# A wider opening, feature-map folds as small products, and finer side steps in a fused attention and SwiGLU kernel

## The chip, the cores and the metric

The kernel runs on one core of a Trainium2 chip. The metric is the device time of one execution in microseconds (us); lower is better. TensorE (PE in the profile) multiplies, VectorE (DVE) and ScalarE (ACT) do element work and read the matmul results in PSUM, GpSimd (POOL) does element work between SBUF tensors only, and SyncE (SP) issues almost all DMAs. Each engine works through its own queue in order.

## The reference, cut to what matters

Two branches read the same normalised tokens `xn` (2048 tokens, 1024 wide): a linear attention with a learned softmax feature map over 32 heads of width 32, and a gated SwiGLU block with 3584 hidden features. The result is `x + attention * silu(swiglu)`, all in float32.

```python
xn = layernorm(x)                                   # 2048 x 1024
q, k, v = split(xn @ wqkv)                          # 32 heads of 32
pq = einsum("bhsd,hdf->bhsf", q, w_phi)             # per head 32 x 32; pk alike
phi = concat([softmax(p), softmax(-p)])
o = phi_q (phi_k^T v) / (phi_q sum(phi_k));  s = o @ wo
h = silu(xn @ w1) * (xn @ w3)                       # 1024 -> 3584
g = silu(h @ w2)                                    # 3584 -> 1024
out = x + s * g
```

Since `q @ w_phi` is `xn @ (wq @ w_phi)` for each head, the kernel multiplies ("folds") `w_phi` into `wq` and `wk` once, before it uses them.

## The kernel before

**Products.** A float32 operand is held as a high part, rounded to the fast format, and a low part, the rest (`split`, L93 to L96: a ScalarE cast makes the high part, a VectorE subtraction the low part). A product takes three passes (high by high, high by low, low by high). The gate and up projections are done by Winograd's form of Strassen's scheme: 512 of 1024 input columns, 512 tokens, and `w1` beside `w3` give a two by two block product, which seven half-size products cover. Their left sides are sums of four token blocks: A11 and A12 (the first 512 tokens, both halves of the columns), A21 and A22 (the next 512), S1 = A21 + A22, S2 = S1 - A11, S3 = A11 - A21, S4 = A12 - S2. Their right sides come from one block of 128 features: B11 and B21 are the halves of `w1`, and T2, T1, T3, B22 and T4 need `w3` as well (`b_sums`, L128, makes two of the sums). One such product is a *step* of `gate_up` (L628): 12 matmuls of 128x512 at L655.

**Order.** For each half of the tokens (`tb`) there are 28 feature blocks `f` with seven products `j` each, 196 steps. The list `events` gives the order of (tb, f, j); j counts A11, A12, S2, S1, S3, S4, A22. Block 0 and 1 are interleaved (`FIRST_PAIR`), later ones follow one by one. All five queues are written out in program order. The right sides of a step are made four steps ahead (`LEAD`, `prep_at`, `sums_at`), their raw weights are loaded two blocks ahead into two buffers (`rw`, L259).

**Opening.** The first 14 steps come while the tokens are still being loaded, normalised (`stats`, `rstd`, `norm`), turned by TensorE (`turn`, L220, four 128x128 transposes into one PSUM bank, `tr`), copied out (ScalarE) and split. Twenty transposes of no use go ahead of all (L749). Steps 0 to 3 need A11 and A12 only. Between them TensorE does 12 of the 32 folds (`first_folds`, L332): four matmuls each against a block-diagonal `bd` (L252), a ScalarE copy and a store. S2 is made and split ahead of S1 (L803 to L811).

**Side work.** From step 14 on, VectorE, ScalarE and SP do work for later stages between the steps: the operands of the second token half (`side_x`), the other folds (`side_fold`: 16 or 32 small matmuls of 32x32 tiles at L532, turned back by VectorE at L538; two units for the rest of `wk`, eight for `wq`), the operands of the key and value products (`side_kv`), stores (`side_store`). `room` (L438) places each item in the first step whose planned VectorE time stays under 2.55 us. `at` puts an item behind the matmuls of a step. `side_fold` holds all three `tr` banks and bank a from its matmuls (L532) to its transposes.

Behind the two token halves come the key and value heads, the query heads, the second SwiGLU product and the output; these stages are the same in both kernels.

## Time and profile before

| | |
|---|---|
| median of 3 runs (lowest to highest) | 2372.14 us (2369.02 to 2375.39) |
| profiled execution, its own time | 2372.7 us |
| its span in the profile | 2370.9 us |
| mean granted TensorE clock | 0.997 |
| TensorE busy | 2345.3 us, 99% |
| VectorE busy | 1774.7 us, 75% |
| ScalarE busy | 897.9 us, 38% |
| GpSimd busy | 257.6 us, 11% |
| DMA | 578.03 MB, 244 GB/s in the mean |

The span is what the profile covers of the execution; 1.8 us lie around it. The busy time of TensorE includes stretches in which matmuls overlap, and its ends are modelled. A row of a timeline gives the start in us, the time it took, the engine, the line of the kernel, the operation, the tiles (written <- read), the shapes and how many instructions were merged, with idle time before it and what ended it in brackets.

### The profile page before, as it was taken

The page shows a single profiled execution, that of the slowest core. Times are in us where ns is not written, and L with a number is a line of the kernel's source. Part 1 is how long each engine was busy: PE and PEld are TensorE (multiplying, and loading weights), DVE is VectorE, ACT ScalarE, POOL GpSimd, SP SyncE. Part 2 cuts the span into 40 slices and gives each one's busy share as a digit, 9 for nine tenths or more (in the row PEclk, how much of TensorE's full clock was granted, in tenths as well). Part 3 has the DMA queues.
Part 4 walks back from the last instruction along what each step waited for, and adds up shares of the span by engine and source line. Part 5 has one row for each costly group of instructions (what it writes and reads, how often), then busy time and mean ns, then how long its engine had stood idle before and what let it go on. Part 6 is the DMA issues. An engine that isn't in the chain of part 4 may idle for free.

```text
span 2370.9 us, 37641 instructions
## 1 busy us (share of the span) xinstructions
PE 2345.3 (99%) x14592; PEld 1922.2 (81%) x14592; DVE 1774.7 (75%) x2777; ACT 897.9 (38%) x1577; POOL 257.6 (11%) x243
## 2 busy tenths in 40 slices
PE   7999999999999999999999999999999999999999
PEld 6788888888888888888788888887888888888787
DVE  8877778886788888874566666777678888787775
ACT  6545444443455455542221222334443333352000
POOL 1000000000000000000000000331012222113562
PEclk9999999999999999999999999999999999999999
DMA  5446689998988888865987878986444653478763
GB/s 215 149 162 218 227 278 310 320 313 281 281 297 297 293 271 301 272 226 191 377 287 287 293 251 316 369 299 249 160 133 143 204 178 133 164 239 281 205 180 103
DMA packets 298354, 578.03 MB, mean 244 GB/s; under 512 B 24624, under 2 KB 151744, under 8 KB 295488
## 3 DMA queue, kind: packets, MB, share of 16 engines
q1 hardware_dynamic: 291840, 552.56, 69.2%
q10 hardware_dynamic: 6336, 23.07, 2.4%
q8 instruction: 115, 1.88, 0.3%
q14 instruction: 63, 0.52, 0.1%
HBM read 372.64 MB, written 202.91 MB: 243 GB/s over the span
## 4 chain that ended last, share of the span: by engine, by line
PE 93%; DVE 3%; DMA 2%; ACT 1%; issue 0%; POOL 0%; SPq 0%; DVEq 0%; ACTq 0%; POOLq 0%
PE bankb L655 24%; PE bankb L1279 13%; PE bankc L655 12%; PE pm L1431 8%; PE bankb L874 7%; PE bankc L1279 6%; PE banka L655 6%; PE bankc L874 3%; PE banka L1279 3%; PE bankb L941 3%; PE banka L874 2%; PE bankc L941 1%; PE po L1416 1%; PE pkv L859 1%; DMA xoA<-xo_d0A 1%; PE banka L941 1%
## 5 line engine op out<-in xcount | busy, mean ns | idle before, releaser
L96 DVE TENSOR_TENSOR bo<-rw,bo 128x512 fp32r<-128x512 f32 x336 | 231.6, 691 | 151.6 <-ACT bo L95 151.3
L1279 PE MATMUL bankb<-bo,as 128*128 128x512 f32 x960 | 235.2, 389 | 1.3 <-ACT acc L1285 1.3
L1279 PEld LDWEIGHTS bankb<-bo,as 128*128 128x128 f32 x960 | 180.1, 188 | 39.1 <-ACT acc L1285 1.7
L95 ACT CAST bo<-rw 128x512 fp32r<-128x512 f32 x336 | 206.7, 618 | 13.4 <-DMA w_d6B<-w2o 3.3
L655 PE MATMUL bankc<-op0S,bo 128*128 128x512 f32 x672 | 163.2, 392 | 0.3 <-DVE op0S L96 0.3
L655 PE MATMUL bankb<-op0S,bo 128*128 128x512 f32 x672 | 162.1, 390 | 1.3 <-ACT op0S L95 0.6
L655 PE MATMUL bankb<-op1S,bo 128*128 128x512 f32 x672 | 161.4, 389 | 0.9 <-ACT u L690 0.9
L655 PE MATMUL bankc<-op1S,bo 128*128 128x512 f32 x672 | 161.5, 389 | 0.1
L655 PE MATMUL bankb<-op0A,bo 128*128 128x512 f32 x672 | 160.6, 394 | 0.7 <-ACT op0A L738 0.7
L1431 PE MATMUL pm<-wos,oT 128*128 128x512 f32 x672 | 160.0, 393 | 0.0
L851 POOL MEMSET ev<- 128x32 f32 x32 | 4.2, 132 | 1419.2 <-DVE bo L96 1083.8
L1279 PE MATMUL bankc<-bo,as 128*128 128x512 f32 x624 | 158.4, 389 | 0.0
L655 PE MATMUL bankb<-op1A,bo 128*128 128x512 f32 x672 | 157.7, 390 | 0.0
L655 PEld LDWEIGHTS bankb<-op0A,bo 128*128 128x128 f32 x672 | 126.5, 190 | 28.2 <-ACT op0A L738 1.1
L655 PEld LDWEIGHTS bankc<-op0S,bo 128*128 128x128 f32 x672 | 125.0, 188 | 29.9 <-issue 2.5
L655 PEld LDWEIGHTS bankb<-op0S,bo 128*128 128x128 f32 x672 | 125.6, 188 | 28.0 <-DVE op0S L96 1.1
L655 PEld LDWEIGHTS bankb<-op1S,bo 128*128 128x128 f32 x672 | 126.0, 188 | 27.5 <-ACT u L690 1.3
L655 PEld LDWEIGHTS bankb<-op1A,bo 128*128 128x128 f32 x672 | 125.8, 188 | 27.5 <-DVE u L698 1.3
L655 PEld LDWEIGHTS bankc<-op1S,bo 128*128 128x128 f32 x672 | 126.0, 188 | 26.6 <-DVE bo L96 0.5
L1431 PEld LDWEIGHTS pm<-wos,oT 128*128 128x128 f32 x672 | 124.8, 188 | 27.4 <-DVE oT L1422 0.3
L1279 PEld LDWEIGHTS bankc<-bo,as 128*128 128x128 f32 x624 | 117.1, 188 | 24.4
L1293 DVE TENSOR_TENSOR acc<-bankb,acc 128x512 f32<-128x512 f32 x152 | 102.0, 685 | 31.2 <-PE bankb L1279 31.2
(272 smaller groups left out, 4333.9 us busy)
## 6 DMA issues: line engine op xcount, KB each, us to landing
rw<-in_w SPq DMA_DIRECT2D x112, 512.0 KB, 4.5
hr<-h_d SPq DMA_DIRECT2D x56, 512.0 KB, 5.4
h_d<-h SPq DMA_DIRECT2D x111, 256.0 KB, 4.9
xoS<-xo_d0S SPq DMA_DIRECT2D x44, 512.0 KB, 6.5
xoS<-xo_d1S SPq DMA_DIRECT2D x44, 512.0 KB, 5.7
xoA<-xo_d0A SPq DMA_DIRECT2D x33, 512.0 KB, 5.2
xoA<-xo_d1A SPq DMA_DIRECT2D x33, 512.0 KB, 4.4
e_d<-eq ACTq DMA_DIRECT2D x32, 512.0 KB, 6.1
```

Of the source, the lines that this page charges most:

```text
L95: nc.scalar.copy(hi, src)
L96: (by or nc.vector).tensor_sub(lo, src, hi.bitcast(F))
L655: nc.tensor.matmul(bank[b], bos[tb, f][bn][:, w, k], ao[an][:, u, k], start=first and n == 0, stop=LAST[b] == an and n == 11, skip_group_c ...
L851: nc.gpsimd.memset(v[:, :, DH:], 1.0)
L859: nc.tensor.matmul(pkv[sl, m], e[:, m // 4, (m % 4) * P + 32 * h:(m % 4) * P + 32 * h + 32], v[:, 4 * (m % 4) + h], start=first and m == 0 ...
L874: nc.tensor.matmul(bank[b], xo[an][:, u, k], wb[bn][:, w, k], start=an in ("A11", "A12", "S1") and n == 0, stop=LAST[b] == an and n == 11, ...
L941: nc.tensor.matmul(bank[b], xo[an][:, u, k], wb[bn][:, w, k], start=an in ("A11", "A12", "S1") and n == 0, stop=LAST[b] == an and n == 11, ...
L1279: nc.tensor.matmul(bank[b], t[:, u, pos + k], bos[kb, bn, k][:, w], start=first and n == 0, stop=LAST[b] == an and n == 5, skip_group_chec ...
L1293: nc.vector.tensor_add(c, pb, c)
L1416: nc.tensor.matmul(po[32 * j:32 * j + 32, a, 64 * k:64 * k + 64], kvs[sl, j, c, k], et[sl, :, 4 * k + j], start=True, stop=True, skip_grou ...
L1431: nc.tensor.matmul(p, oTs[t, h][:, a, k], wos[c, 4 * h + k][:, b], start=n == 0, stop=n == 3 * ND - 1)
```

## The change

The opening covers four feature blocks in place of two, so that steps 0 to 8 (except step 7) need only the token blocks A11 and A12 and the `w1` halves of blocks 0 to 3; blocks 2 and 3 get their right sides B11 and B21 from raw weights put into an unused part of an operand buffer, and a `tr` bank each for their bank b (`kept_banks`). S1 is made and split ahead of S2. Seven low parts of the opening (`first_b` with `nc.gpsimd`) and `b_sums` of blocks 0 and 1 are on GpSimd; in the kernel before only those `b_sums` were. Sixteen more transposes go ahead. The 12 folds against `bd` are gone from the opening; all folds are 16 units of `side_fold` of 16 matmuls each, every one with its own load, transposes and store through one buffer `wf`. The side items of two VectorE instructions become items of one, and the starts of the side work (`FIRST_STEP`, `KV_STEP`, `UNITS`) are new. The three `tr` banks have a name each (`tr_bank`). `wkT` comes from the host in the layout of `wqT`.

```diff
+    def b_sums(b11, b12, b22, t2, eng=None, parts=range(2)):
 
         eng = eng or nc.vector
-        eng.tensor_sub(b12, b22, b12)
-        eng.tensor_add(t2, b12, b11)
+        if 0 in parts:
+            eng.tensor_sub(b12, b22, b12)
+        if 1 in parts:
+            eng.tensor_add(t2, b12, b11)
...
+    turned, kept_banks = [0], {}
+
+    def tr_bank():
+
+        while True:
+            turned[0] += 1
+            if turned[0] % 3 not in kept_banks.values():
+                return dict(tag=f"tr{turned[0] % 3}", bufs=1)
+
+    def turn(half, **kw):
+        pt = ps.tile([P, 4, P], F, name="pt", **(kw or tr_bank()))
...
-    def load_w(wT, dch, c, t=None):
-        wr = blk("wr") if t is None else t
-        nc.sync.dma_start(wr, wT[dch][:, 4 * c:4 * c + 4])
-        return wr
-
-    def fold(wr, c):
-
-        pw = ps.tile([P, 4, P], F, name="pw", tag="tr", bufs=3)
-        for g in range(4):
-            nc.tensor.matmul(pw[:, g, :], wr[:, g], bd[:, 4 * c + g, :], start=True, stop=True)
-        return pw
-
-    folds = [(wkT, k, c, wk_d[c][k]) for c in range(2) for k in range(ND)][:FOLDS]
...
+    def b_operand(bo, n, src, by=None):
+        bo[n] = quad("bo")
+        split(bo[n][:, 0], bo[n][:, 1], src.rearrange("p (k n) -> p k n", n=P), by)
...
+    def b_others(rw, bo, t2=None):
+
+        b11, b21, b12, b22 = rw
+        late = t2 is None
+        if late:
+            t2 = work.tile([P, 512], F, name="t2", tag="w")
+            b_sums(b11, b12, b22, t2)
             yield
         else:
-            hold.append(lambda: b_sums(b11, b12, b22, t2, eng))
-        for _, _, n in ORDER:
-            src = {"B11": b11, "B21": b21, "T2": t2, "T1": b11, "T3": b12, "B22": b22, "T4": b21}[n]
-            bo[n] = quad("bo")
-            split(bo[n][:, 0], bo[n][:, 1], src.rearrange("p (k n) -> p k n", n=P))
-            if n == ("B11" if hold is None else "T2"):
+            nc.vector.tensor_sub(b11, b22, t2)
+        for n in ("T2", "T1", "T3", "B22", "T4") if late else ("T1", "T2", "T3", "B22", "T4"):
+            b_operand(bo, n, {"T2": t2, "T1": b11, "T3": b12, "B22": b22, "T4": b21}[n])
+            if n == "T2" and late:
                 nc.vector.tensor_sub(b11, b22, t2)
-            elif n == ("B21" if hold is None else "B22"):
+            elif n == ("T1" if late else "T3"):
                 nc.vector.tensor_sub(b21, b21, t2)
             yield
...
-    FIRST_PAIR = ((0, 0), (1, 0), (0, 1), (1, 1)) + tuple((f, j) for j in range(2, 7) for f in range(2))
-    events = [(0, f, j) for f, j in FIRST_PAIR] + [(0, f, j) for f in range(2, NF) for j in range(7)]
+    OPENING = ((0, 0), (1, 0), (0, 1), (2, 0), (1, 1), (3, 0), (2, 1), (0, 3), (3, 1), (1, 3), (0, 2), (1, 2))
+    OPENING += tuple((f, j) for j in range(4, 7) for f in range(2)) + tuple((f, j) for f in range(2, 4) for j in range(2, 7))
+    events = [(0, f, j) for f, j in OPENING] + [(0, f, j) for f in range(4, NF) for j in range(7)]
...
-            elif tb == 0 and f < 3:
-                steps = ([0, 0, 0, 4, 5, 5, 6], [0, 0, 0, 4, 6, 8, 9], [11, 12, 13, 14, 15, 16, 16])[f]
+            elif tb == 0 and f < 4:
+                steps = ([8, 9, 10, 11], [8, 10, 12, 13], [15, 16, 16, 17, 18], [19, 20, 21, 22, 23])[f]
...
-            at_ = room(at_ + 1, 1.3)
-            at(at_, lambda j=j: stats(mv[0], j, xt[j]))
+            for h in range(2):
+                at_ = room(at_ + 1, 0.75 if h else 0.61)
+                at(at_, lambda j=j, h=h: half_stats(j, h))
...
-        w, banks = [flat(bd)], []
-        if m < 2:
-            gs_, nd = (4 + 2 * m, 5 + 2 * m), 4
-        else:
-            gs_, nd = (m - 2,), ND
+        w, banks, g = [], [], m % G
+        src, dst = (wkT, wk_all) if m < G else (wqT, wq_all)
 
         def load():
-            if m < 2:
-                for n, g in enumerate(gs_):
-                    nc.sync.dma_start(w[0][:, 512 * n:512 * n + 512].rearrange("p (d n) -> p d n", d=4),
-                                      wkT[4:, :, g].rearrange("d p n -> p d n"))
-            else:
-                nc.sync.dma_start(w[0], wqT[gs_[0]])
+            w.append(bdp.tile([P, G * P], F, name="wf"))
+            nc.sync.dma_start(w[0], src[g])
 
         def multiply():
-            banks.extend(ps.tile([P, 512], F, name="pf", tag="tr", bufs=3) for _ in range(3))
+            banks.extend(ps.tile([P, 512], F, name="pf", **tr_bank()) for _ in range(3))
             banks.append(ps.tile([P, 512], F, name="banka", bufs=BANKS["a"]))
-            for n, g in enumerate(gs_):
-                wn = w[0][:, 512 * n:512 * n + P * nd].rearrange("p (d k) -> p d k", d=nd)
-                for q in range(4):
-                    for j in (3, 0, 1, 2):
-                        sl = slice(32 * j, 32 * j + 32)
-                        nc.tensor.matmul(banks[j][32 * q:32 * q + 32, P * n:P * n + 32 * nd], phi_raw[sl, g], wn[sl, :, 32 * q:32 * q + 32],
-                                         start=True, stop=True, skip_group_check=True)
+            wn = w[0].rearrange("p (d k) -> p d k", d=ND)
+            for q in range(4):
+                for j in (3, 0, 1, 2):
+                    sl = slice(32 * j, 32 * j + 32)
+                    nc.tensor.matmul(banks[j][32 * q:32 * q + 32, :32 * ND], phi_raw[sl, g], wn[sl, :, 32 * q:32 * q + 32],
+                                     start=True, stop=True, skip_group_check=True)
 
         def turn(j):
-            for n in range(len(gs_)):
-                o = w[0].rearrange("p (d n f) -> p d n f", d=nd, f=DH)[:, :, 4 * n + j]
-                nc.vector.transpose(o, banks[j][:, P * n:P * n + 32 * nd].rearrange("p (d f) -> p d f", f=DH))
+            o = w[0].rearrange("p (d n f) -> p d n f", d=ND, f=DH)[:, :, j]
+            nc.vector.transpose(o, banks[j][:, :32 * ND].rearrange("p (d f) -> p d f", f=DH))
 
         def store():
-            if m < 2:
-                d = wk_late.rearrange("d p n -> p d n")[:, :, 256 * m:256 * m + 256]
-            else:
-                d = wq_all[gs_[0] // 4].rearrange("d p n -> p d n")[:, :, P * (gs_[0] % 4):P * (gs_[0] % 4) + P]
-            nc.sync.dma_start(d, w[0].rearrange("p (d n) -> p d n", d=nd))
+            nc.sync.dma_start(dst[g // 4].rearrange("d p n -> p d n")[:, :, P * (g % 4):P * (g % 4) + P],
+                              w.pop().rearrange("p (d n) -> p d n", d=ND))
...
-        at(at_ + 2, store)
-        fold_free[0] = at_ + 4
+        at(at_ + 1, store)
+        fold_free[0] = at_ + 3
...
-    FIRST_STEP = 14
+    FIRST_STEP, KV_STEP = 16, 82
+    UNITS = (33, 40, 47, 60, 74, 81, 95, 102, 109, 116, 123, 130, 137, 144, 151, 158)
+    for m, s0 in enumerate(UNITS):
...
-            if paired and b == "a":
-                bank[b] = ps.tile([P, 512], F, name="banka", tag="tr", bufs=3)
+            if paired and b == "a" or tb == 0 and f in (2, 3) and b == "b":
+                bank[b] = ps.tile([P, 512], F, name=f"bank{b}", **tr_bank())
+                if b == "b":
+                    kept_banks[f] = turned[0] % 3
...
-                if step < 4:
+                if step < 9:
...
+    first_rws, pts = [rws.pop(0) for _ in range(2)], {}
+    for f in range(4):
         bos[0, f] = {}
-        gens[0, f] = b_operands(rws.pop(0), bos[0, f], nc.gpsimd, held)
-    pts = {}
+
+    def first_b(f, n, by=None):
+        b_operand(bos[0, f], ("B11", "B21")[n], raw_b[f][:, n], by)
 
     def early_at(t, h):
         n = ("A11", "A12")[h]
@@ -744,78 +743,77 @@
     def early_raw(t, h):
         raw[t][early_at(t, h)[0]] = raw_x(pts.pop((t, h)))
 
+    in_c = dict(tag="bankc", bufs=BANKS["c"])
     nc.scalar.activation(sds[0][:, 1, :1], eps_t, AF.Sqrt)
     warm = ps.tile([P, 512], F, name="banka", bufs=BANKS["a"])
-    for k in range(20):
+    for k in range(36):
         nc.tensor.transpose(warm[:, :P], xs[2 + min(k // 8, 1)][k // 4 % 2][:, k % 4 * P:k % 4 * P + P], ident)
     for t in range(4):
         stats(mvs[0], t, xs[t])
-    _, sd = rstd(mvs[0], sds[0], lambda: next(gens[0, 0]))
+    _, sd = rstd(mvs[0], sds[0], lambda: first_b(0, 0))
     for t in range(4):
         norm(mvs[0], sd, t, xs[t], (0,))
-        early_turn(t, 0, **(dict(tag="bankc", bufs=BANKS["c"]) if t == 3 else {}))
+        early_turn(t, 0, **(in_c if t == 3 else {}))
+    nc.gpsimd.tensor_copy(consts[:, 1:2], xs[3][0][:, 0:1])
+    first_b(1, 0, nc.gpsimd)
+    first_b(0, 1, nc.gpsimd)
     for t in range(4):
         early_low(t, 0)
-    next(gens[0, 1])
     reads = [gate_up(0)]
     for t in range(4):
         early_raw(t, 0)
     for t in range(4):
         norm(mvs[0], sd, t, xs[t], (1,))
-    next(gens[0, 0])
+    first_b(1, 1, nc.gpsimd)
+    stats(mvs[1], 0, xs[4])
     for t in range(4):
-        early_turn(t, 1, **(dict(tag="bankc", bufs=BANKS["c"]) if t == 0 else {}))
+        early_turn(t, 1, **(in_c if t == 0 else {}))
     for t in range(4):
         early_low(t, 1)
     reads.append(gate_up(1))
     reads[0]()
     for t in range(4):
         early_raw(t, 1)
-    stats(mvs[1], 0, xs[4])
-    next(gens[0, 1])
     reads[1]()
+    first_b(2, 0, nc.gpsimd)
     reads.append(gate_up(2))
-    first_folds(2)
-    first_copies(2)
-    stats(mvs[1], 1, xs[5])
-    reads[2]()
     reads.append(gate_up(3))
-    first_folds(4)
-    load_folds(2)
-
-    nc.gpsimd.tensor_copy(consts[:, 1:2], mvs[1][:, 0, 0:1])
-    for do in held:
-        do()
-    held.clear()
-    for t in range(2, 4):
+    for t in range(1, 4):
         stats(mvs[1], t, xs[4 + t])
+    for f in range(2):
+        rw, t2 = first_rws.pop(0), work.tile([P, 512], F, name="t2", tag="w")
+        b_sums(rw[0], rw[2], rw[3], t2, nc.gpsimd)
+        gens[0, f] = b_others(rw, bos[0, f], t2)
+    del rw, t2
     r1 = rstd(mvs[1], sds[1])
     next(r1)
-    first_copies(4)
-    load_folds(2)
+    reads[2]()
+    reads.append(gate_up(4))
     sd = next(r1)
+    first_b(3, 0, nc.gpsimd)
+    reads[3]()
     for t in range(4):
         norm(mvs[1], sd, t, xs[4 + t])
     for t in range(4, 8):
-        first_turn(t, 0)
-        first_turn(t, 1)
-    load_folds(2)
-    reads[3]()
-    first_sums("S1", (0, 1))
-    first_sums("S2", (0, 1))
-    first_split("S2", (0, 1))
-    first_folds(3)
-    first_copies(2)
-    first_sums("S1", (2, 3))
-    first_sums("S2", (2, 3))
-    first_split("S2", (2, 3))
+        first_turn(t, 0, **(in_c if t % 2 else {}))
+        first_turn(t, 1, **(in_c if t % 2 else {}))
+    reads.append(gate_up(5))
+    first_b(2, 1, nc.gpsimd)
+    first_b(3, 1, nc.gpsimd)
+    reads[4]()
+    reads.append(gate_up(6))
+    for qs in ((0, 1), (2, 3)):
+        first_sums("S1", qs)
+        first_split("S1", qs)
     next(gens[0, 0])
-    first_folds(2)
-    first_copies(2)
+    reads[5]()
+    reads[6]()
+    reads.append(gate_up(7))
     next(gens[0, 1])
-    first_folds(1)
-    first_copies(2)
-    assert first_folds.at == FOLDS and not to_copy
+    for qs in ((0, 1), (2, 3)):
+        first_sums("S2", qs)
+        first_split("S2", qs)
+    reads[7]()
 
     def first_late(n):
         ao[n] = slot(0, ANAMES.index(n))
@@ -825,14 +823,13 @@
         for h in silus:
             nc.scalar.activation(h, h, AF.Silu)
 
-    at(4, lambda: first_split("S1"))
-    at(5, first_silus)
-    at(5, lambda: first_sums("S3"))
-    at(6, lambda: first_late("S3"))
-    at(7, lambda: first_sums("S4"))
-    at(8, lambda: first_late("S4"))
-    at(9, lambda: first_late("A22"))
-    for step in range(4, len(events)):
+    at(9, first_silus)
+    at(8, lambda: first_sums("S3"))
+    at(9, lambda: first_late("S3"))
+    at(10, lambda: first_sums("S4"))
+    at(11, lambda: first_late("S4"))
+    at(12, lambda: first_late("A22"))
+    for step in range(8, len(events)):
```

141 lines of the change are left out of this document (67 added, 74 removed).

## Prediction

> **What bounds the kernel now.** I read the page first, then the waits of TensorE, then its timeline over the opening.
>
> ```profile
> PE 2345.3 (99%) x14592; PEld 1922.2 (81%) x14592; DVE 1774.7 (75%) x2777; ACT 897.9 (38%) x1577; POOL 257.6 (11%) x243
> PE 93%; DVE 3%; DMA 2%; ACT 1%; issue 0%; POOL 0%; SPq 0%; DVEq 0%; ACTq 0%; POOLq 0%
> ```
>
> TensorE is busy for 99% of the span and is 93% of the chain that ended last. The end moves only by matmul work taken out or put in, and by time in which TensorE waits or runs slowly. The waits of TensorE from 68 to 600 us have one row:
>
> ```profile
> PE bankc L655 <- DVE op0S L96: 0.3, 1, 0.3
> ```
>
> From 68.5 us to 600 us nothing makes it wait: side work there is free as long as it stays hidden, and what the opening gains arrives at the end. The opening, as TensorE's timeline:
>
> ```profile
> 7.08 4.00 PE L750 MATMUL banka<-ident,xt 128*128 128x128 f32 x20 [7.08 <-DMA xt<-in_x]
> 13.27 3.21 PE L223 MATMUL pt<-ident,xt 128*128 128x128 f32 x16 [2.19 <-DVE xt L218]
> 17.16 4.64 PE L655 MATMUL bankb<-op0A,bo 128*128 128x512 f32 x12 [0.68 <-ACT op0A L738]
> 21.64 1.91 PE L223 MATMUL pt<-ident,xt 128*128 128x128 f32 x16
> ...
> 37.48 3.94 PE L223 MATMUL pt<-ident,late_x 128*128 128x128 f32 x32
> ...
> 60.84 0.73 PE L655 MATMUL bankb<-op0S,bo 128*128 128x512 f32 x2 [0.64 <-ACT op0S L95]
> 62.22 5.29 PE L655 MATMUL bankb<-op0S,bo 128*128 128x512 f32 x22 [0.64 <-DVE op0S L96]
> ...
> 68.24 5.28 PE L655 MATMUL bankc<-op0S,bo 128*128 128x512 f32 x22 [0.29 <-DVE op0S L96]
> 73.36 8.32 PE L655 MATMUL bankb<-op0A,bo 128*128 128x512 f32 x36
> 81.52 2.88 PE L655 MATMUL banka<-op0A,bo 128*128 128x512 f32 x12
> 84.24 2.88 PE L655 MATMUL bankb<-op0S,bo 128*128 128x512 f32 x12
> ```
>
> A step takes 2.72 us (81.52 to 84.24). The row at 73.36 holds steps 12, 13 and 14, so step 13, the 14th, ends at 73.36 + 2 x 2.72 = 78.8 us. After it both kernels do the same matmuls, apart from fold units; this is the mark that I compare. The granted clock, in windows of 1 us (us; PE busy and instructions; PEclk; DMA share; GB/s):
>
> ```profile
> 12.00:13.00 1.00, 0.00 (x0) 1.00 1.03 422
> 13.00:14.00 1.00, 0.73 (x6) 0.92 1.03 418
> 14.00:15.00 1.00, 1.00 (x6) 0.50 1.02 418
> 20.00:21.00 1.00, 1.00 (x5) 0.67 1.06 408
> ```
>
> The clock falls to 0.50 just behind the 2.19 us wait and comes back after 20 us. So the first step takes 4.5 us (17.16 to 21.64) and the first four turns 0.80 each (3.21 / 4), against 1.91 / 4 = 0.48 at 21.64.
>
> **The change, part by part.** The folds that go, those that come, and the prices of the other engines:
>
> ```profile
> L252 PE MATMUL pw<-bd,room_b 128*128 128x128 f32 x64 | 8.0, 277 | 0.0
> L252 PE MATMUL pw<-bd,wr 128*128 128x128 f32 x32 | 4.2, 278 | 1.9 <-ACT room_b L343 1.9
> 183.31 2.88 PE L655 MATMUL bankb<-op0S,bo 128*128 128x512 f32 x12
> 187.12 3.03 PE L655 MATMUL bankc<-op0S,bo 128*128 128x512 f32 x12
> 189.99 0.39 PE L655 MATMUL bankb<-op0S,bo 128*128 128x512 f32 x1
> 310.18 2.88 PE L655 MATMUL bankb<-op0S,bo 128*128 128x512 f32 x12
> 313.63 3.01 PE L655 MATMUL bankc<-op0S,bo 128*128 128x512 f32 x12
> 316.49 0.84 PE L655 MATMUL bankb<-op0A,bo 128*128 128x512 f32 x3
> 312.99 0.40 PE L532 MATMUL banka<-bd,early_z 32*32 32x256 f32 x1
> L538 DVE STREAM_TRANSPOSE bd<-pf x36: 272/407/444, 196.2 to 496.2; 128x256 f32<-128x256 f32 x24, 128x128 f32<-128x128 f32 x12
> 24.66 2.12 ACT L228 COPY xf<-pt 128x512 f32<-128x512 f32 x4
> 41.49 0.69 ACT L228 COPY xf<-pt 128x512 f32<-128x512 f32 x1
> 54.75 1.28 ACT L826 ACT_TABLE_LOAD   x1
> 51.82 2.49 DVE L96 TENSOR_TENSOR op0S<-room_b,op0S 128x512 fp32r<-128x512 f32 x4
> 12.67 1.92 DVE L218 TENSOR_SCALAR xt<-xt,consts 128x512 f32<-128x512 f32 x4
> 35.12 3.74 DVE L218 TENSOR_SCALAR late_x<-late_x,consts 128x512 f32<-128x512 f32 x8
> 27.09 1.28 POOL L131 TENSOR_TENSOR rw<-rw 128x512 f32<-128x512 f32 x1
> 27.32 1.60 DVE L96 TENSOR_TENSOR bo<-rw,bo 128x512 fp32r<-128x512 f32 x1 [0.51 <-ACT bo L95]
> 28.45 1.60 POOL L132 TENSOR_TENSOR t<-rw 128x512 f32<-128x512 f32 x1
> 418.00:478.00 60.00, 59.99 (x321) 48.23 (x320) 48.99 (x80) 27.52 (x52) 0.00 (x0) 1.00 0.94 316
> ```
>
> *Folds.* The 12 of the opening are 12.2 us of TensorE (8.0 + 4.2). Two steps with an old key unit between them last 189.99 - 183.31 = 6.68, so the unit costs 6.68 - 5.44 = 1.24; a query unit 6.31 - 5.44 = 0.87. Before: 2 x 1.24 + 8 x 0.87 = 9.4. After: 16 x 0.87 = 13.9. The units cost 4.5 more, behind the mark, where TensorE never waits: on the path in full.
>
> *Prices in the opening.* ScalarE 0.5 an operation (2.12 / 4), VectorE 0.60 for two inputs (2.49 less its first start, over 4), 0.47 for a normalisation (3.74 / 8), GpSimd 1.3. A two-input VectorE operation that met a GpSimd one took 1.60: it began at 27.32, GpSimd ended at 28.37, and 0.55 later it was done; GpSimd's next took 1.60 in its turn. So the two take turns and each holds the other for its whole length.
>
> *Clock and step 0.* The 16 added transposes last 1.9 us at the warm pace (1.91 for 16) or 3.2 at that of L750 (4.00 / 20 each): they end between 13.0 and 14.3, and the first turn, which waits for VectorE, comes at 13.27. That costs 0 to 1.0; I take 0, since the wait at 13.27 is then filled and the clock stays up. Then turns and casts go at 0.5: high parts done at 16.0 (17.1 before). VectorE's normalisations end at 14.6, its four lows at 17.0. Step 0 runs from 16.0 to 19.3, because its third matmul needs the last low. Before: 21.6. Gain 2.3. By the Trainium skill (TensorE: Matmul & The Clock Gate, Part 1: The HAM clock gate), the clock is judged in free-running windows of about 3.4 us, and an idle one halves it; the trace agrees (down near 13.9, up two such windows later, near 20.6). By that rule the sum is the same if a window ends at 13.9 again, and an estimate of up to 1.0 less where one ends later, since the added transposes then run cold.
>
> *Steps 1 to 6.* Normalisations end at 18.9, four turns run from 19.3 to 21.2, steps 1 to 4 to 32.1 (4 x 2.72, and 0.2 for block 2's low part from GpSimd), eight late turns to 36.0 (3.94), steps 5 and 6 to 41.4. These two replace folds as filler. GpSimd's seven low parts and four sums hide under the steps: each is wanted 1 us or more after its end, bar the one above.
>
> *Step 7, the new wait.* It needs all of S1 and T1. ScalarE finishes the eight copies at 36.8 (4.7 after the turns begin, as from 37.48 to 42.18), then has two casts for blocks 2 and 3 and two for S1: 38.8. On VectorE the first S1 low waits for GpSimd's low part of block 2 until 38.65, and the second for that of block 3: 1.5 us of holding; two sums, two lows, one subtraction, cast and low of T1 follow: 44.65 for the high part, 45.25 for the low. Step 7 runs from 44.65 to 47.75. TensorE waits 3.2 + 0.4 us. Queued behind on VectorE are S2 and T2, so later steps wait as well.
>
> *Steps 8 to 13.* Steps 8 to 11 follow without a gap to 58.6. VectorE has 24 operations from T1's low to the last S3 low: 24 x 0.6 + 1.0 of handovers = 15.4, to 60.65. ScalarE's table load and four SiLUs (1.28 + 4 x 0.5) lie ahead of S3's casts; step 12 must wait for the copy of step 10's result, which is in ScalarE's queue behind these casts and three more operations: 61.75. Step 12 ends at 64.5; step 13 waits for the like copy behind S4's casts (seven more VectorE operations): 66.0 to 68.7. TensorE waits 3.1 + 1.5 here. From here VectorE is ahead again: A22's lows end near 71, step 16 starts at 74.
>
> *At nothing:* the side items, singly or in pairs the same instructions; VectorE has 11 of 60 us free in the fullest stretch (48.99 of 60.00). Eight whole key units for two half ones add 32 transposes of 0.41 less 16 of 0.27, 9 us, over 450. If this cover were gone, the loss would be what VectorE falls behind. Reload of the block 2 weights waits for block 0's T4 and has 6 us before VectorE needs it. On SP the folds' 24 transfers leave the opening; two loads of raw `w1` go ahead of the `w3` halves, which nobody wants before 26 us. The kept `tr` banks are free again at step 27, when the first side tile is turned.
>
> *Sum.* Mark 78.8 - 68.7 = 10.1 gained, 4.5 given back: 5.6. Against the profiled execution's 2372.7: 2367.1. That execution is 0.6 above the median of the runs, 2372.14, so the forecast is **2366.5**. Its own range is 2363.5 to 2369.5: 1.0 for the transposes, 1.5 for the holding, and the 0.5 by which each of four long chains may be off.
>
> **Rivals.**
>
> *Shorter waits.* The kernel before also makes and splits four sums here, and TensorE waited 0.64 + 0.64 + 0.29 = 1.6 us behind step 7, not 4.6. If the new order waits no more, and GpSimd has its low parts done before S1's (no holding, 1.5), 3.0 + 1.5 come on top: 2362.0. For it: the rows at 60.84 to 68.24. Against it: the counted queue, in which the copies stand behind the casts.
>
> *Normalisations are held too.* They take 0.47 for 512 columns where a two-input operation takes 0.60, so they run in another mode, and no row shows one beside GpSimd. Held like the operation at 27.32, the four at 17 us alternate with GpSimd's three low parts and end at 22.2, not 18.9; the tiny ones of the second variance stand between the `b_sums`, and the late turns start at 35.9, not 32.1. The mark comes at 72.2, 3.5 later: **2370.0**. By the Trainium skill (SBUF — State Buffer, Who interferes with whom), a VectorE instruction in a two-port mode, which it says a tensor-scalar can enter, and one with two SBUF inputs exclude GpSimd, each for the whole instruction; for the second kind the row at 27.32 agrees, for the first no row here can tell.
>
> *Slower: the units starve.* All 16 units load, and store, through one buffer. Their load now waits for the store before it and is planned 3 steps ahead for most, 4 or 5 before:
>
> ```profile
> 300.80 0.35 SPq L522 DMA_DIRECT2D bd<-in_wqT  x1
> DMA to landing us min/median/max: 3.0/5.6/9.1
> ```
>
> One load 3 steps ahead was issued at 300.80 for the unit at 313.0: 12.2 us, over the 9.1 of the slowest landing. If the denser SP queue issues it over 3 us later, TensorE waits; 2 us at each of 12 units are 24: **2390**. The point where it turns: issue to landing plus lateness above 12.2. For it: DMA share 0.94 already at 418. Against it: the 3 us of room.
>
> *It does not do what it says:* the clock falls all the same. Then step 0 ends 2.3 later: 2368.8.
>
> **How the numbers follow.** Forecast 0.35, shorter waits 0.28, normalisations held 0.13, starving units 0.18, clock 0.06. The bound is 0.3% of 2372.14, 7.1 us, about what a measurement of this kernel tells from no change: faster is below 2365.0, slower above 2379.3. Faster: 0.28 and a third of the forecast, 0.12: 0.40. Slower: 0.18. Within: 0.42. The range 2359 to 2378 leaves out the starving units and the end of the shorter waits, 0.2.
>
> **What would show it.** Right: granted clock 1.0 from 13 to 21 us; step 0 ending near 19; waits of 3 us before the first S1 product and before S3's; the 14th step done near 69; units of 0.87. Wrong: normalisations of over 1 us beside GpSimd; waits at the units' matmuls; TensorE waiting behind 80 us.

## Result and profile after

The changed kernel takes 2386.03 us (median of 4 runs, 2383.86 to 2390.39) against 2371.79 us (2369.02 to 2375.39) for the kernel before: ratio 1.0061, 95% interval 1.0042 to 1.0081. It is slower; the forecast was 2366.5. The profiled execution took 2386.1 us, its span is 2384.0.

The page after (busy time by engine):

```profile
PE 2345.6 (98%) x14640; PEld 1916.0 (80%) x14640; DVE 1781.1 (75%) x2786; ACT 893.6 (37%) x1565; POOL 264.6 (11%) x245
```

TensorE is busy as long as before (2345.3 us): 12.8 of the 13.1 us by which the span has grown are, in the balance, time in which it stands idle. It is a balance: TensorE has less work of folds (12.2 us gone, 4.5 added), but more transposes ahead, and it runs stretches at half clock that it did not have. TensorE's timeline after; the rows are the end of step 0, the late turns, steps 5 to 8 and 12 to 17:

```profile
17.82 2.54 PE L650 MATMUL bankb<-op0A,bo 128*128 128x512 f32 x10 [0.32 <-DVE op0A L741]
...
35.92 3.87 PE L232 MATMUL pt<-ident,late_x 128*128 128x128 f32 x32 [1.26 <-issue]
39.54 3.01 PE L650 MATMUL bankb<-op0A,bo 128*128 128x512 f32 x12
...
48.62 0.50 PE L650 MATMUL bankc<-op0S,bo 128*128 128x512 f32 x1 [3.25 <-ACT bo L93]
49.35 4.38 PE L650 MATMUL bankc<-op0S,bo 128*128 128x512 f32 x11 [0.23 <-DVE bo L94]
53.56 2.88 PE L650 MATMUL banka<-op0A,bo 128*128 128x512 f32 x12
...
66.46 3.01 PE L650 MATMUL bankb<-op0S,bo 128*128 128x512 f32 x12 [1.85 <-ACT u L686]
72.54 4.61 PE L650 MATMUL bankb<-op0S,bo 128*128 128x512 f32 x12 [3.07 <-ACT u L686]
76.99 5.60 PE L650 MATMUL bankc<-op0S,bo 128*128 128x512 f32 x24
82.43 5.60 PE L650 MATMUL bankb<-op0A,bo 128*128 128x512 f32 x24
```

The mark, the end of the 14th step, lies at 76.99 us: 1.8 earlier than before (78.8), not 10.1. Two steps there take 4.4 (a row of 11 of its 12 matmuls) and 4.6 us for 2.7. Later, where the kernel before had no wait from 68.5 to 600 us, two waits of TensorE are new (us in total, times, longest), and so are two at the switch of the token halves:

```profile
PE banka L526 <- DMA wf<-in_wqT: 4.9, 1, 4.9
PE banka L526 <- DVE rw L276: 0.8, 1, 0.8
```

```profile
396.89 4.92 PE L650 MATMUL bankb<-op0S,bo 128*128 128x512 f32 x12
...
609.12 2.79 PE L650 MATMUL bankb<-op1A,bo 128*128 128x512 f32 x11 [1.45 <-DVE bo L94]
638.39 3.78 PE L650 MATMUL bankc<-op1S,bo 128*128 128x512 f32 x11 [1.77 <-DVE bo L94]
```

VectorE's waits for weights at the switch, before (L131) and after (L130):

```profile
DVE rw L131 <- DMA rw<-in_w: 2.7, 1, 2.7
DVE room L131 <- DMA room<-in_w: 5.1, 1, 5.1
...
DVE rw L130 <- DMA rw<-in_w: 4.4, 1, 4.4
DVE room L130 <- DMA room<-in_w: 6.8, 1, 6.8
```

I follow four points through all kernels: the start of step 16, of the first product of the second token half, of the first product of the key and value heads, and the span (all us, from the profiled execution), beside the median time.

| kernel | step 16 | second half | heads | span | median | ratio to before (95%) |
|---|---|---|---|---|---|---|
| before | 84.24 | 591.61 | 1127.26 | 2370.9 | 2371.8 | |
| changed | 82.43 | 601.85 | 1141.98 | 2384.0 | 2386.0 | 1.0061 (1.0042 to 1.0081) |
| gpsimd_moved | 77.44 | 597.01 | 1135.37 | 2378.4 | 2379.5 | 1.0034 (1.0022 to 1.0046) |
| scalar_order | 78.14 | 596.62 | 1137.04 | 2379.4 | 2383.4 | 1.0047 (1.0035 to 1.0059) |
| fold_gap | 81.60 | 595.24 | 1133.15 | 2375.6 | 2378.4 | 1.0031 (1.0019 to 1.0043) |
| switch_only | 80.53 | 599.71 | 1134.98 | 2377.7 | 2379.7 | 1.0033 (1.0023 to 1.0044) |
| no_products | 81.63 | 586.82 | 1125.55 | 2370.9 | 2373.0 | 1.0004 (0.9995 to 1.0013) |
| before_36_warm | 81.97 | 589.29 | 1124.37 | 2368.4 | 2370.2 | 0.9993 (0.9984 to 1.0002) |
| all_three | 74.40 | 585.66 | 1124.04 | 2366.9 | 2369.0 | 0.9991 (0.9982 to 1.0000) |
| s4_on_gpsimd | 73.28 | 584.75 | 1125.67 | 2367.2 | 2370.2 | 0.9999 (0.9990 to 1.0008) |
| load_ahead | 75.48 | 586.70 | 1124.40 | 2367.8 | 2369.1 | 0.9993 (0.9984 to 1.0002) |
| t1_early | 70.96 | 582.52 | 1122.30 | 2364.5 | 2367.4 | 0.9976 (0.9966 to 0.9987) |
| all_five | 70.91 | 583.09 | 1117.91 | 2360.8 | 2363.4 | 0.9963 (0.9950 to 0.9976) |

From before to changed, the span grows by 13.1: -1.8 up to step 16, +12.0 from there to the second half (519.42 instead of 507.37), +4.5 from there to the heads (540.13 instead of 535.65), -1.6 behind them. That last part is the same in all these kernels and takes 1241.5 to 1245.4 us in their executions, so 1.6 there means nothing. The first transposes start between 6.96 and 8.08 us in these executions, when the first tile has landed, and 36 of them take 5.61 to 7.09 us; differences of 1 us at step 16 can come from each of these alone.

### The profile page after: what moved, and what is told of

Read it like the earlier page. It is cut to its first block, busy times and chain, and to the rows that moved or that the text cites. A ratio compares the mean times of both kernels' runs of the same rounds, so it can differ in the third digit from the quotient of the medians.

```text
span 2384.0 us, 37741 instructions
## 1 busy us (share of the span) xinstructions
PE 2345.6 (98%) x14640; PEld 1916.0 (80%) x14640; DVE 1781.1 (75%) x2786; ACT 893.6 (37%) x1565; POOL 264.6 (11%) x245
## 4 chain that ended last, share of the span: by engine, by line
PE 89%; DMA 4%; DVE 3%; ACT 1%; issue 1%; SPq 0%; POOL 0%; DVEq 0%; ACTq 0%; POOLq 0%
PE bankb L650 23%; PE bankb L1276 13%; PE bankc L650 11%; PE pm L1428 8%; PE bankb L871 7%; PE bankc L1276 6%; PE banka L650 5%; PE bankc L871 3%; PE banka L1276 3%; PE bankb L938 3%; PE banka L871 2%; PE bankc L938 1%; PE po L1413 1%; PE pkv L856 1%; DMA xoA<-xo_d0A 1%; PE banka L938 1%
## 5 line engine op out<-in xcount | busy, mean ns | idle before, releaser
L94 DVE TENSOR_TENSOR bo<-rw,bo 128x512 fp32r<-128x512 f32 x329 | 226.0, 688 | 143.9 <-ACT bo L93 143.2
L650 PE MATMUL bankb<-op0S,bo 128*128 128x512 f32 x672 | 167.1, 399 | 4.9 <-ACT u L686 4.9
```

What stands on the lines that cost most here:

```text
L94: (by or nc.vector).tensor_sub(lo, src, hi.bitcast(F))
L650: nc.tensor.matmul(bank[b], bos[tb, f][bn][:, w, k], ao[an][:, u, k], start=first and n == 0, stop=LAST[b] == an and n == 11, skip_group_c ...
```

## The experiments

**1. GpSimd's operations elsewhere.**

```diff
+    first_cast(1, 0); first_cast(0, 1)      # ahead of the first normalisations
...
-    first_b(1, 1, nc.gpsimd)
+    gate_pool(xs[3][1])                     # GpSimd waits for the second normalisations
+    first_low(1, 1); first_low(2, 0); first_b_sums(0)
...
+    first_low(3, 0); first_low(2, 1)
...
-    b_sums(rw[0], rw[2], rw[3], t2, nc.gpsimd)   # blocks 0 and 1, behind the statistics
+    gate_pool(xs[7][1])                     # behind the late normalisations
+    first_low(3, 1); first_b_sums(1)
```

> The changed kernel with GpSimd's eleven operations of the opening put elsewhere, nothing else: two low parts from 15.4 us (their casts done earlier), then held back until the second normalisations are done, three more low parts and two sums beside the statistics, the last low part and two sums only behind the late normalisations. Theory (GpSimd holds VectorE): the second normalisations take 2.0 to 2.5 us instead of 4.61, the small operations of the second variance 0.16 to 0.2 each instead of 0.73 to 1.21, the first two S1 lows 1.3 instead of 2.55; step 7 starts 4 to 5 us earlier (44 to 44.6 instead of 48.62), its wait falls under 2 us and with it the half clock behind it; the 14th step ends at 70.5 to 73 instead of 77.0, and the time is 2380 to 2382 us. Rival (ScalarE's queue before S3's and S4's steps sets the end of the opening): step 7 starts as much earlier, but the waits before steps 12 and 13 (1.85 and 3.07) grow by as much; the 14th step ends after 75.5, the time is 2384 to 2386.

VectorE's timeline of the changed kernel: the second normalisations, one small operation of the second variance, the late normalisations, the first two S1 lows.

```profile
17.68 4.61 DVE L218 TENSOR_SCALAR xt<-xt,consts 128x512 f32<-128x512 f32 x4
31.75 1.21 DVE L210 SCALAR_TENSOR_TENSOR consts<-consts 128x4 f32<-128x4 f32 x1
34.36 4.65 DVE L218 TENSOR_SCALAR late_x<-late_x,consts 128x512 f32<-128x512 f32 x8
42.18 2.55 DVE L94 TENSOR_TENSOR op0S<-room_b,op0S 128x512 fp32r<-128x512 f32 x2 [1.37 <-ACT op0S L93]
```

The same with GpSimd moved, and TensorE's step 7:

```profile
16.88 1.98 DVE L218 TENSOR_SCALAR xt<-xt,consts 128x512 f32<-128x512 f32 x4
28.26 0.16 DVE L210 SCALAR_TENSOR_TENSOR consts<-consts 128x4 f32<-128x4 f32 x1
28.86 3.74 DVE L218 TENSOR_SCALAR late_x<-late_x,consts 128x512 f32<-128x512 f32 x8
```

```profile
42.51 0.49 PE L650 MATMUL bankc<-op0S,bo 128*128 128x512 f32 x1 [1.30 <-ACT bo L93]
...
66.42 5.49 PE L650 MATMUL bankb<-op0S,bo 128*128 128x512 f32 x12 [3.06 <-ACT u L686]
71.71 5.89 PE L650 MATMUL bankc<-op0S,bo 128*128 128x512 f32 x24
```

The theory stands: on VectorE the same instructions, but the normalisations take 1.98 us for 4.61, the small operation 0.16 for 1.21; step 7 comes 6.1 us earlier, 5.3 of them against fold_gap (47.83), whose first tile landed at the same time. Of these 5.3, 3.05 lie ahead of the late turns (32.07 against 35.12) and 1.2 in the first two S1 lows (1.35 us for 2.56). The other 1.1 are not GpSimd's: the edit also moves two casts of ScalarE, which stood ahead of S1's, to an earlier place. The 14th step ends at 71.7 and the time falls by 6.5 us, 1.8 of it at the switch. The half clock behind step 7 is gone, the one in step 13 has become longer (5.49), and the wait before step 12 has grown from 1.85 to 2.83 us, so the rival is right in part.

**2. Which operations hold each other.** A stretch of VectorE operations behind the end of the kernel: three of a kind alone, then eight beside four GpSimd operations.

```diff
+    for do in (norms, two_sbuf, one_psum, bn, small_two, turned_psum):
+        for g in (g_two, g_copy):
+            for k in range(3): do(k)
+            nc.vector.tensor_copy(gp[2][:, 0:1], src[2][:, 0:1])     # lets GpSimd start
+            for k in range(4): g(k)
+            for k in range(8): do(k)
+            nc.vector.tensor_copy(src[2][:, 1:2], gp[1][:, 1:2])     # waits for it
```

> The changed kernel with a stretch of measurements behind its end: six kinds of VectorE operation, three of each alone and then eight of each beside four GpSimd operations, once two-input subtractions and once copies (128x512 f32). Theory (the two engines exclude each other for whole operations when VectorE reads two inputs from SBUF or runs its fast normalisation): the normalisation takes 0.48 us alone and up to 1.6 beside GpSimd, the subtraction of two SBUF inputs 0.6 alone and up to 1.6, the small 128x4 product 0.16 alone and up to 1.3; the subtraction from PSUM, the statistics and the transposition from PSUM are the same alone and beside it. Rival (only the bandwidth of memory is shared): every kind grows by the same share, the small one hardly.

VectorE's timeline there (normalisations alone and beside; two SBUF inputs beside; one PSUM input beside), and GpSimd's row beside the subtractions with two SBUF inputs; then the small product by line (shortest, median, longest in ns):

```profile
2387.21 1.32 DVE L1500 TENSOR_SCALAR dst<-src,sc 128x512 f32<-128x512 f32 x3
2388.51 7.51 DVE L1500 TENSOR_SCALAR dst<-src,sc 128x512 f32<-128x512 f32 x8
...
2404.18 4.89 DVE L1503 TENSOR_TENSOR dst<-src,src 128x512 f32<-128x512 f32 x8
...
2424.21 4.86 DVE L1506 TENSOR_TENSOR dst<-pp,src 128x512 f32<-128x512 f32 x8
```

```profile
2404.41 9.45 POOL L1518 TENSOR_TENSOR gp<-gp,gp 128x512 f32<-128x512 f32 x4 [3.72 <-DVE gp L1527]
```

```profile
L1512 DVE TENSOR_TENSOR tiny<-sc x22: 149/159/1239, 2449.9 to 2457.1; 128x4 f32<-128x4 f32 x22
```

Eight normalisations take 7.51 us beside GpSimd, where three alone take 1.32; the small product goes up to 1.24; subtractions with an input from PSUM, statistics and transposes from PSUM are not held (eight take 4.86, 4.84 and 2.75 us, three alone 1.87, 1.87 and 1.10). That part of the theory stands, and the rival of shared bandwidth falls. One part fails: eight subtractions of two SBUF inputs in a row were not held at all (4.89); GpSimd was, with 9.45 us for four. By the Trainium skill (SBUF — State Buffer, Who interferes with whom) an operation that has the shared ports keeps them for its whole length and issue order decides who blocks. The kinds that are held agree with it; that a row of VectorE operations keeps GpSimd out for several of them is what this run adds.

**3. The order on ScalarE.**

```diff
-    at(9, first_silus)
+    at(13, first_silus)
-    at(11, lambda: first_late("S4"))
-    at(12, lambda: first_late("A22"))
+    at(12, lambda: first_late("S4"))
+    at(13, lambda: first_late("A22"))
```

> The changed kernel with another order on ScalarE alone: the four SiLUs with their table load come 4 steps later, S4's and A22's split one step later each. Theory (the bank copies of steps 10 and 11 stand behind the SiLUs and casts): the waits before steps 12 and 13 (1.85 and 3.07 us) fall to under 1 us in sum, the half clock at 73 us goes, the 14th step ends at 71 to 72.5 instead of 77.0, the time is 2380 to 2382 us. Rival (VectorE's row of 24 operations is the bound there): the third products of S3's and S4's steps wait for their low parts, which end at 65.4 and 73.0 as now; what is won at the 14th step is lost by the 17th, the time 2384.5 to 2386.

TensorE's timeline: the first row of these holds the rest of step 12 and step 13.

```profile
65.18 5.32 PE L650 MATMUL bankb<-op0S,bo 128*128 128x512 f32 x22 [0.23 <-DVE op0S L94]
71.66 0.73 PE L650 MATMUL bankc<-op0S,bo 128*128 128x512 f32 x2 [1.16 <-ACT op0S L93]
73.00 5.30 PE L650 MATMUL bankc<-op0S,bo 128*128 128x512 f32 x22 [0.61 <-DVE op0S L94]
```

The copies of steps 10 and 11 no longer wait behind SiLUs and casts: steps 12 and 13 run through, and the half clock of step 13 goes. 1.8 us of waits come back at step 14 for S4, as the rival had it, but step 16 starts at 78.14, 4.3 earlier than in the changed kernel. The time, 2383.4, lies between theory and rival; the profiled execution, 2381.5, is 1.9 under it.

**4. The fold units further apart.**

```diff
-    UNITS = (33, 40, 47, 60, 74, 81, 95, 102, 109, 116, 123, 130, 137, 144, 151, 158)
+    UNITS = (33, 40, 47, 60, 74, 81, 95, 102, 109, 123, 130, 137, 144, 151, 158, 165)
```

> The changed kernel with one edit: the fold units from the 11th on come 7 steps later (start steps 123, 130, ... 165 instead of 116, 123, ... 158), so that the one load that was issued behind a late store has 7 more steps. Theory (one starved unit): the wait of 4.9 us at 391 us and the half clock behind it (a step of 4.92 instead of 2.88) go, the first product of the second token half comes 6.5 to 7 us earlier (601.85 to about 595), and the time is 2379 +-2 us against 2386. Rival (the units as such cost more than their 0.87 each, and another load is late in its place): a wait at another unit, the first product of the second token half within 2 us of 601.85, the time 2384 to 2387.

The changed kernel's last two transposes of the 10th unit on VectorE; on SP's queue the row ahead of its store, the store, and the load of the 11th; then TensorE's waiting unit, there and with the gap:

```profile
377.28 0.77 DVE L531 STREAM_TRANSPOSE wf<-pf 128x256 f32<-128x256 f32 x2
```

```profile
381.10 2.98 SPq L441 DMA_DIRECT2D wkv_d1T<-wkvo  x1
384.18 0.56 SPq L534 DMA_DIRECT2D wq_d<-wf  x1
391.73 0.35 SPq L517 DMA_DIRECT2D wf<-in_wqT  x1
```

```profile
395.80 0.60 PE L526 MATMUL banka<-wf,early_z 32*32 32x256 f32 x1 [4.89 <-DMA wf<-in_wqT]
```

```profile
410.58 0.37 PE L526 MATMUL banka<-wf,early_z 32*32 32x256 f32 x1 [2.28 <-DMA wf<-in_wqT]
```

The 10th unit was multiplied at 370.91, and VectorE had turned it back by 378.05, 7.1 us later. Its store came only at 384.18: it stood on SP behind other stores, the last of which took 2.98 us, 2.6 of it a wait for VectorE. The load of the 11th then had to wait for the store to land, 7.5 us, and went out at 391.73, when TensorE already stood idle. (The edit moves the 10th and all later ones; the expectation counts one too far.) With it the transposes take as long, but the store follows them at once, 7.2 us behind the products, and the wait of the 11th falls from 4.89 to 2.28 us, without a half clock behind it. The second half starts 6.6 us earlier, 0.8 of it from an earlier first tile, and the time falls by 7.6; 2.2 us of that come at the switch (537.91 for 540.13), which the edit does not touch. The next run has a longer gap behind the 10th unit too, and there the last wait is gone.

**5. The three edits together**, with two gaps instead of one (units at ... 109, 123, 137, 144 ... 172).

> The changed kernel with the three edits together: GpSimd's operations moved, the SiLUs and the splits of S4 and A22 later, the fold units further apart (the 10th at step 123, the 11th at 137, then every 7 steps, which gives 7 steps more to the unit that still waited 2.28 us). Theory (three separate losses): the gains of the single edits add up, 6.5 + 2.6 + 7.6 and 2.3 for the last starved unit: 2386.0 - 19.0 = 2367 +-2, and faster than the kernel before by 4 us. Rival (VectorE is late in both parts of the opening, so that two of the edits win the same time): the 14th step not before 68, the time 2370 to 2373, no faster than the kernel before.

Step 16 starts at 74.40 and the second half at 585.66: the stretch between is 511.26, no unit waits, and the 4.5 us forecast for the units are 511.26 - 507.37 = 3.9. The time is 2369.0, 17.0 under the changed kernel: the three single gains sum to 16.7, and with the last starved unit 19.0 were expected, so it lies at the edge of that range. The rival falls, since the 14th step has ended before 66.4. The 4 us under the kernel before are not there: 0.9991 (0.9982 to 1.0000) is level with it.

**6. The units without their products.**

```diff
         def multiply():
-            for q in range(4): ... nc.tensor.matmul(banks[j]...)
+            pass
         def turn(j):
-            nc.vector.transpose(o, banks[j]...)
+            pass
```

> The changed kernel without the 256 products and the 64 transpositions of its fold units: their loads and stores stay where they are, so the key and query weights are stored unfolded. Theory (the units' products lie on TensorE's path in full, 0.87 each, and beside them only the starved unit counts): 16 x 0.87 = 13.9 us less, 4.9 + 0.8 of waits and about 2 of half clock: 2386.0 - 21.6 = 2364.4 +-2. Rival (VectorE, which loses 64 transpositions of 0.41 = 26 us of work, was late in the side stage or at the switch of the token halves, and TensorE with it): also the waits at the switch go, 4 us more: below 2361.

The waits from 360 to 500 us, ScalarE's and TensorE's:

```profile
ACT h L693 <- DMA h_d<-h: 14.2, 3, 5.3
ACT wkvo L93 <- DMA wkv_d1T<-wkvo: 4.6, 1, 4.6
PE bankb L642 <- ACT u L678: 2.6, 5, 1.1
```

It fell by 13.1 us only. Both theories were wrong: from 360 to 480 us the transfers are full (DMA share 1.05; 1.02 in the changed kernel), and with less for TensorE to do, ScalarE waits for stores to free its buffers and TensorE for ScalarE. The stretch to the second half is 505.19; taking 13.9 out of 511.26 would be 497.4. The 42 steps from 372.23 to 494.34 us take 122.1 us where 42 x 2.72 are 114.2: 7.9 us go to such waits. So about half of the products' time lies where TensorE would have waited for transfers.

**7. The warming transposes alone**, in the kernel before.

```diff
-    for k in range(20):
+    for k in range(36):
         nc.tensor.transpose(warm[:, :P], ...)
```

> The kernel before with 36 warming transpositions instead of 20, as in the changed kernel, and nothing else. Theory (the fall of the clock comes from the 2.19 us without matmuls before the first turn): granted clock 1.0 from 13 to 21 us, step 0 ends at 19.3 to 20 instead of 21.6; in this kernel VectorE's row sets the rest of its opening, so by the late turns the gain is used up: the 14th step at 78 to 78.8, the time 2370 to 2371.5. Rival (TensorE sets the opening): the gain reaches the end, 2369 to 2369.7. Second rival (the clock falls all the same): nothing moves, 16 more transpositions at the slow clock push the first turn 0.5 to 1 us later.

```profile
13.12 2.02 PE L223 MATMUL pt<-ident,xt 128*128 128x128 f32 x16
...
16.97 2.58 PE L655 MATMUL bankb<-op0A,bo 128*128 128x512 f32 x10 [0.32 <-DVE op0A L742]
```

The wait before the first turn is gone, step 0 ends at 19.4 and not 21.6. The 2.3 us are still there at step 16 and at the second half: my theory that VectorE would use them up falls, the first rival holds in the trace. The time, 0.9993 (0.9984 to 1.0002), cannot tell it from nothing.

**8. S4's sums on GpSimd.**

```diff
-                nc.vector.tensor_sub(flat(a[n]), flat(a["A12"]), flat(a["S2"]))
+                nc.gpsimd.tensor_sub(flat(a[n]), flat(a["A12"]), flat(a["S2"]))
```

> The kernel with all three edits (2369.0 us), and the four S4 sums (128x512, two inputs from SBUF) on GpSimd instead of VectorE, which is busy without a gap from 43 to 67 us. Theory (VectorE's row sets steps 12 to 15 there; beside it GpSimd gets its turns): VectorE is 2.5 us ahead from 61.5 on, S4's casts start by 62, the waits before step 14 (1.18 and 0.61 us) and the half clock behind them (1.6 us) go: 2366 +-1. Rival (while VectorE runs two-input subtractions back to back, GpSimd gets no turn, as in the measured stretch where one of its operations took 5.8 us, or each holds the other): the sums end after 66, S4's casts start later than 64.1, the waits before step 14 grow by 1 to 4 us: 2369 to 2373.

GpSimd took 3.37 and 3.33 us for two sums each, VectorE 3.31 and 3.28 for two lows beside them: each holds the other, as in the rival. TensorE waited 1.77 and 1.82 us at step 10 instead of at step 14, and ran at half clock behind that. Step 16 starts 1.1 us earlier than in all_three, but 0.8 of that is there at step 7 already, ahead of the edit. The stretch from the second half to the heads takes 540.92 us for 538.38, with waits for VectorE of 1.85 and 2.13. Nothing is won (2370.2).

**9. The switch of the token halves.** First one load on SP in the kernel of experiment 5 (load_ahead), then in the changed kernel both edits (switch_only):

```diff
-   load_at.setdefault(steps[-1] + 1, []).append(late)
+   ... if late != (1, 1) else at(steps[-1], lambda: rws.append(b_load(1)))
...
         at(s0, load)                       # side_w
-        at_ = s0 + 4
+        at_ = s0 + (4 if u else 7)
```

> The kernel with all three edits (2369.0 us), and on SyncE's queue one load moved: the two transfers of the weights of block 1 of the second token half go ahead of the second four of the eight transfers that reload S2 and S1 at the switch, not behind them. Theory (these weights come late because they stand behind the reloads, which go out at the pace of the transfers, 1.4 us each): they are issued 5 to 8 us earlier, VectorE waits under 1 us for them instead of 3.75, TensorE's wait behind the switch (0.83 us and the 0.63 us at the next) goes, from the first product of the second token half to the first of the K and V heads 536 to 537 us instead of 538.4, the time 2367 to 2368. Rival (the transfers are full there, whatever the order): the reloads come later by as much, TensorE waits for S2 or S1 instead: 2369 to 2370.

> The changed kernel (2386.0 us) with two edits at the switch of the token halves and none elsewhere: the weights of block 1 of the second half are loaded ahead of the second four reloads, and the sums of the first of the later weight units come 3 steps later on VectorE, behind the landing of their loads (VectorE waited 6.8 us for them in line, TensorE 1.77 us behind that, then at half clock). Theory (the 4.5 us that the changed kernel loses between the first product of the second half and the first of the K and V heads come from these two transfers that VectorE waits for in line): the stretch takes 535 to 536 us as in the kernel before, instead of 540.1; the time 2381 to 2382.5 us. Rival (the change lost them in the work that follows, where the side work now goes in single steps): the stretch still takes over 537.5, the time 2384 to 2386.

The load alone takes the first wait away (issued 11.7 us ahead of the second half, not 5.2), while the second grows to 1.07: 537.70 instead of 538.38 from the second half to the heads, and a time that does not move (2369.1). With both edits the stretch is 535.27 in the changed kernel, as before the change (535.65); the time falls by 6.4 us, of which 4.9 are this stretch. The theory stands: these two waits are what the change lost at the switch.

**10. A version that beats both.** To the edits of 5 and the load of 9 comes T1's work of blocks 0 and 1 in VectorE's idle time before the S1 sums (t1_early); all_five adds the other edit of 9.

```diff
+    first_t1(0)                            # b11 = b22 - t2, at 33 us
     reads.append(gate_up(5))
...
         first_sums("S1", qs)
+        if 0 in qs: next(gens[0, 0])       # cast and low part beside the sums
         first_split("S1", qs)
```

> The kernel with all three edits and the load ahead of the reloads (2369.1 us), and T1's work of blocks 0 and 1 put where VectorE has idle time: the subtraction of block 0 at 32.5 us (its two inputs have been there since 25), its cast and low part beside the S1 sums, the subtraction of block 1 ahead of the S2 sums. Theory (VectorE's row from the late turns to step 15 sets the opening): step 7 starts at the end of step 6, 1.3 us earlier, VectorE is 2 us earlier at S3 and S4, the waits before step 14 shrink or the half clock of 1.6 us behind them goes: 2366 to 2367.5. Rival (what is won before step 7 is lost at the next copies and casts): step 16 starts within 0.5 us of where it did, 2368.5 to 2369.5.

> All edits together (the last stood at 2367.35 us), now with the sums of the first later weight unit 3 steps later. Theory: the wait of 3.01 us at the switch and the half clock of 1.5 us behind it go: 2363 to 2364.5 us, under the kernel before by more than 0.3%. Rival (work moved from a place where VectorE waited to one where it is full): the stretch from the switch to the heads stays over 537 us, the time 2366 to 2368.

TensorE's step 7 and its neighbour in all_five:

```profile
39.01 2.88 PE L650 MATMUL banka<-op0A,bo 128*128 128x512 f32 x12
42.22 3.29 PE L650 MATMUL bankc<-op0S,bo 128*128 128x512 f32 x12 [0.33 <-ACT op0S L93]
```

Step 7 follows step 6 with a wait of 0.33, step 16 starts 13.3 us earlier than before the change, and nothing waits from there to the heads but 0.65, 0.27 us. t1_early is at 2367.4 (with another 3.01 us at the switch), all_five at 2363.4 us, 0.9963 of the kernel before. Part of this is chance: step 16 starts 3.5 us earlier in all_five than in all_three, whose late turns start at the same time, and 1.6 of that is a half clock that did not follow the same waits before step 14.

## Why the prediction was wrong, step by step

The forecast for the span was 5.6 less, it came out 13.1 more. The 18.7 us between are 8.3 at the mark, 7.5 on the way to the second half, 4.5 at the switch, less 1.6 behind the heads.

*Clock and step 0: right.* The granted clock stays up where it fell before (windows of TensorE: us, busy and instructions, granted clock, DMA share, GB/s):

```profile
13.00:14.00 1.00, 1.00 (x11) 1.00 1.03 422
14.00:15.00 1.00, 1.00 (x10) 1.00 1.01 414
20.00:21.00 1.00, 1.00 (x10) 1.00 0.48 172
```

And experiment 7 sizes the gain at the 2.3 us forecast. Step 0 ended at 20.2 instead of 19.3 because the first tile landed later in this execution.

*Steps 1 to 6: the step that failed first.* The late turns were put at 32.1 and came at 35.92; 0.9 of that is the first tile, 2.9 the normalisations and the small operations of the second variance, which GpSimd holds. The step that failed priced a normalisation at 0.47 us with GpSimd at work beside it: the four at 17.68 took 4.61, not 1.9. The rival "normalisations are held too" named the mechanism, and 35.9 us for the late turns; that it fits to the digit is luck, for 0.9 of the delay is the first tile. I gave it 0.13 since no row of before showed a normalisation beside GpSimd; experiment 2 shows the price, 0.94 on average for 0.44.

*Step 7's wait: right, its consequence missing.* Forecast 3.2 + 0.4, measured 3.25 + 0.23. But the clock fell behind it (the same view):

```profile
49.00:50.00 1.00, 0.77 (x3) 0.71 0.00 0
50.00:51.00 1.00, 1.00 (x4) 0.50 0.00 0
51.00:52.00 1.00, 1.00 (x3) 0.50 0.00 0
52.00:53.00 1.00, 1.00 (x4) 0.58 0.06 16
```

Half clock from 49.42 to 52.84 (0.71 and 0.58 give the edges), 3.4 us, costs half of that, 1.7. I had counted the clock at the start, where the profile showed it fall, and not at the new waits that I forecast myself. The same price was paid in step 13 and at 396.89 (4.92 for 2.88). By the Trainium skill (TensorE: Matmul & The Clock Gate, Part 1: The HAM clock gate) the clock is set by windows of about 3.4 us that run freely. The trace agrees in the length. It agrees, too, in that a half clock is then a matter of chance: behind the same waits before step 14 (1.2 + 0.61) the 22 matmuls took 6.85 us in all_three and 5.28 in t1_early.

*Steps 8 to 13: mechanism right, sizes off.* The waits behind ScalarE's casts were forecast at 3.1 and 1.5 and came at 1.85 and 3.07, 4.9 in all. With the half clock of step 13 (1.8) the lag on the forecast grew from 5.8 us at step 8 to 8.3 at the mark. Experiment 3 shows that the queue was the cause. With it and GpSimd mended, step 16 starts at 74.40, where the prediction had 74: a gain of that size was there, behind two orders of instructions. That the two figures meet is in part luck, since all_three waits 4.5 us from step 7 on and not 8.2, and then loses 1.6 at half clock.

*Fold units: right for the six that were added*, 3.9 for 4.5. That every unit lies on the path in full is not: without the products of all sixteen only 6.1 of 13.9 us went (511.26 in all_three less 505.19 in no_products).

*"The units starve": the rival on the slower side came true in part.* I saw the one buffer and a late SP, but set 12.2 us against the landing of the load alone. The load also waits for the landing of the store before it, 7.5 us, and the store stood 6.1 us on SP behind others. It hit one unit of 16, not 12, and cost 8.2 with its half clock (519.42 - 511.26), not 24.

*"After it both kernels do the same matmuls": too much was read from it.* The switch, which the sum had at nothing, cost 4.5 us. VectorE's order there is the same in both kernels; its two waits for weights lie at the edge of being hidden, 2.7 and 5.1 us before, 4.4 and 6.8 after. The eight reloads ahead of them went out in 10.3 and 10.6 us in the two traces of the kernel before and in 10.8 to 11.9 in those of the changed kernel and its descendants that kept that order. Why they go slower stays open.

*The other rivals.* Shorter waits did not come; the clock did not fall at the start. The side work in single steps was put at nothing; the one sign of it is a wait for VectorE behind the switch, 0.57 us near 644 us in all_three, that neither the kernel before nor the changed kernel has.

## What to carry to other kernels

In these runs work moved to GpSimd was free only beside VectorE's statistics, its transposes and its subtractions with an input from PSUM: place it there, and keep normalisations and small two-input operations clear of it. Count every new wait of TensorE with the half clock that may follow, and look in ScalarE's queue for what stands ahead of the copy that frees a bank. A buffer that is loaded again behind its own store has the store's landing and everything ahead of the store on its path; and where the transfers are full, work taken from TensorE is paid back as waits.

## What the runs showed of the hardware

Beside a row of eight VectorE subtractions with two SBUF inputs one GpSimd operation took 5.8 us that takes 1.26 alone, while the subtractions were not held. Beside normalisations the two took turns (GpSimd 1.40 to 1.44 an operation). A GpSimd copy holds too: eight of the same subtractions took 6.54 us beside four copies. In the kernel two subtractions in a row were held as well (3.28 us for two in s4_on_gpsimd). What decides whether a row of them is held or holds is not shown.
